# Attention memory and feed-forward kernel: the second feed-forward product with the activations stationary and 512 weight columns moving

## The chip, the cores and the metric

One core of one Trainium2 chip runs the whole program. The metric is the device time of one execution in microseconds. Three runs of the kernel before gave 767.05, 767.28 and 768.91; the median is 767.28.

## What is computed

8 batches, 8 heads, 576 tokens of 64 values a head, 32 memory slots; the feed-forward part has 512 inputs, 2048 hidden columns and 512 outputs. All in float32.

```python
a = softmax over tokens (phi)                      # b h s m
k_m = einsum('bhsm,bhsd->bhmd', a, k)
v_m = einsum('bhsm,bhsd->bhmd', a, v)
attn = softmax over m (q @ k_m.T / sqrt(64))       # b h s m
x = (attn @ v_m), heads side by side               # (4608, 512)
h = x @ w_in                                       # (4608, 2048)
sp = maximum(h, 0) + log1p(exp(-abs(h)))           # softplus
g = h * erf(sp)
return g @ w_out                                   # (4608, 512)
```

## The kernel before

**Folding.** `attn @ v_m @ w_in` is computed as `attn @ (v_m @ w_in)`: `vw` multiplies each head's 32x64 `v_m` with `w_in`, and the first product then contracts over 8 heads x 32 slots = 256 rows, in two groups of 128.

**Precision.** Most large products run in fp32r on split operands: `split` makes a high part (ScalarE, L110) and the remainder (VectorE, L111), and `products` forms three matmuls, high x high, high x low, low x high. Batch 0 keeps its first product, and the first 8 steps (`WHOLE`) keep their second product, in plain fp32 with one operand each; in the trace a plain fp32 matmul stands as two records.

**Weights.** `w_in` and `w_out` arrive as 64-bit words in 8 pieces of 1 MB each. `decode_1` and `decode_2` rebuild the floats: a clamp (VectorE L133), two conversions (ScalarE L136, L137), and two bit operations (VectorE L160, L163). `split_wo` later splits `w_out` for the fp32r steps.

**Steps.** `ORDER` lists 128 steps: 16 half batches `u` of 288 tokens, each with 8 steps `c` of 256 hidden columns. In step i:

- `ffn1(i, j)`, j = 0, 1 (L396): 6 matmuls each, vw stationary (128 hidden columns), 288 attention columns moving, into a bank `psh`; VectorE copies it to `h` (L405).
- `softplus` (L413) and, for four steps together, `erf` (L416) on ScalarE; the grouping saves activation table loads.
- `g_split` (L427 to L429) on VectorE, four steps later: e times h, its high part, its low part.
- `ffn2(i - 6, d)` (L444), d = 0 to 3: w_out stationary (128 output columns), g moving (288 tokens), 6 matmuls each, into one of four banks `pso`. After step c = 7 of a half batch ScalarE moves the four banks out (L469) and SyncE stores them (L472). The output is transposed, `outT`.

**The next batch's preparation** is hung on the steps by `at_slot`: the token softmax of phi (`phi_max`, `phi_sub`, `phi_exp`, `phi_sum`), the memory products (`kmvm`, L269, and `block_diag`, L285), `scores` (L302), the slot softmax (`sm_max`, `sm_exp`, `sm_norm`, `sm_back`), and four `vw_pair` (L302, then the split at L110 and L111). Batch 0's preparation stands ahead of step 0, together with the first decodes; this and the steps of batch 0 are called the front here.

**What sets the order.** The program is a list `prog` of (function, arguments); `merge` spreads side tasks between the four `ffn2` of a step. Each engine's instructions may then move only within `WINDOW` of that order: for TensorE freely in the first 16 steps (`HEAD`), then one, that is strictly in order; for VectorE 12, then 4; for ScalarE free, then 4. Loads are issued by SyncE when a buffer of their pool comes free (`room`, `fill`); `FIRST` gives the order of the earliest loads. kv has a ring of 3 buffers, q and phi one each, the weights 8. TensorE's results use 8 banks: two for `psh`, two for all small products (`psa`), four for `pso`.

```python
FIRST = "wo phiT phiT phi raw raw raw start q start wo wo wo wo".split()
...
lhsT=x[:, d * P : (d + 1) * P],   # ffn2: w_out
rhs=y[:, j, :],                   # ffn2: g, 288 tokens
```

## Time and profile before

| what | us |
|---|---|
| median of three runs | 767.28 (767.05 to 768.91) |
| span of the profiled execution, first to last instruction | 764.4 |
| TensorE busy | 728.3 |
| TensorE weight loads busy | 645.1 |
| VectorE busy | 515.9 |
| ScalarE busy | 433.8 |
| GpSimd busy | 0.7 |

The profile holds one execution and its span; the time of that execution around its span is not listed apart, so the span is set beside the median, which is 2.9 us longer. Times are us from the span's start. In groups of instructions, "x1920" counts records and "ns" is the mean length of one; matmuls are pipelined, so their lengths overlap, and the distance from start to start is what one costs. "PE" is TensorE, "PEld" its weight loads, "DVE" VectorE, "ACT" ScalarE, "POOL" GpSimd, "SPq" the queue in which SyncE issues DMAs. In a stretch of the timeline "x8" is eight instructions in a row, and the bracket names the idle time before them and what ended it.

### The profile page before, as it was taken

How to read it: one execution, taken by the hardware profiler on the slowest of the kernel's cores; microseconds unless marked ns; L12 is line 12 of the kernel's file. 1: busy time of each engine (PE TensorE's matmuls, PEld its weight loads, DVE VectorE, ACT ScalarE, POOL GpSimd, SP SyncE). 2: the span in 40 equal slices, each digit the busy share in tenths (PEclk: the TensorE clock that was granted, in tenths of full speed). 3: DMA queues.
4: the chain of work that ended last, by engine and by line, in shares of the span. 5: the costliest groups of instructions: out<-in, count | busy, mean ns of one | idle time of the engine just before them, and what ended most of it. 6: DMA issues, size and time to landing. Idle time of an engine off the chain costs nothing.

```text
span 764.4 us, 14301 instructions
## 1 busy us (share of the span) xinstructions
PE 728.3 (95%) x6016; PEld 645.1 (84%) x6016; DVE 515.9 (67%) x975; ACT 433.8 (57%) x704; POOL 0.7 (0%) x6
## 2 busy tenths in 40 slices
PE   2679899999999999999999999999999999999998
PEld 1245667699989999899999999989998999889998
DVE  3599867776668656777568746776577757667552
ACT  3679785565553746466454755556355755546450
POOL 0000000000000000000000000000000000000000
PEclk9999999999999999999999999999999999999999
DMA  8995042205201250004201151014401011000000
GB/s 295 389 384 245 1 155 63 63 5 180 66 32 33 69 173 32 20 21 154 96 32 32 48 171 47 18 32 126 124 32 32 17 48 32 33 2 32 1 32 32
DMA packets 34367, 64.88 MB, mean 85 GB/s; under 512 B 3072, under 2 KB 22016, under 8 KB 33280
## 3 DMA queue, kind: packets, MB, share of 16 engines
q1 hardware_dynamic: 34304, 63.98, 25.0%
q8 instruction: 47, 0.77, 0.5%
q14 instruction: 16, 0.13, 0.1%
HBM read 54.53 MB, written 9.44 MB: 84 GB/s over the span
## 4 chain that ended last, share of the span: by engine, by line
PE 83%; DVE 8%; ACT 7%; DMA 2%; issue 1%; SPq 0%; ACTq 0%
PE pso L444 50%; PE psh L396 24%; PE psa L302 5%; PE psa L269 3%; DMA phiT<-phiT 1%; DVE w_in L160 1%; ACT w_out L137 1%; ACT e L416 1%; ACT w_out L136 1%; PE psa L285 1%; DVE h L405 1%; DVE w_in L163 1%; ACT e L413 1%; DMA outT<-ot 1%; ACT L413 1%
## 5 line engine op out<-in xcount | busy, mean ns | idle before, releaser
L444 PE MATMUL pso<-g_hi,wo 128*128 128x288 f32 x1920 | 403.6, 295 | 0.1
L444 PEld LDWEIGHTS pso<-g_hi,wo 128*128 128x128 f32 x1920 | 315.0, 188 | 9.3 <-issue 8.3
L444 PE MATMUL pso<-g_lo,wo 128*128 128x288 f32 x960 | 283.4, 295 | 0.0
L444 PEld LDWEIGHTS pso<-g_lo,wo 128*128 128x128 f32 x960 | 180.4, 188 | 2.6 <-issue 1.7
L413 ACT ACTIVATE e<-h 128x576 f32<-128x576 f32 x128 | 86.9, 684 | 155.6 <-DVE h L405 155.2
L405 DVE COPY h<-psh 128x288 f32<-128x288 f32 x256 | 113.9, 450 | 15.7 <-PE psh L396 15.3
L427 DVE TENSOR_TENSOR e<-e,h 128x576 f32<-128x576 f32 x120 | 89.0, 743 | 43.3 <-ACT e L416 43.3
L396 PE MATMUL psh<-at_hi,vw_hi 128*128 128x288 f32 x448 | 101.2, 307 | 0.3 <-ACT at_hi L110 0.3
L396 PE MATMUL psh<-at_lo,vw_hi 128*128 128x288 f32 x448 | 95.7, 295 | 0.4 <-DVE at_lo L111 0.4
L396 PE MATMUL psh<-at_hi,vw_lo 128*128 128x288 f32 x448 | 95.7, 295 | 0.0
L429 DVE TENSOR_TENSOR g_lo<-e,g_hi 128x576 fp32r<-128x576 f32 x120 | 90.1, 751 | 0.5
L396 PEld LDWEIGHTS psh<-at_hi,vw_hi 128*128 128x128 f32 x448 | 70.4, 188 | 22.5 <-issue 16.1
L416 ACT ACTIVATE e<-e 128x576 f32<-128x576 f32 x128 | 80.1, 679 | 0.4
L428 DVE CAST g_hi<-e 128x576 fp32r<-128x576 f32 x120 | 54.4, 453 | 36.0 <-PE pso L444 34.4
L111 DVE TENSOR_TENSOR vw_lo<-psa,vw_hi 128x512 fp32r<-128x512 f32 x56 | 38.4, 686 | 59.1 <-ACT vw_hi L110 59.0
L396 PEld LDWEIGHTS psh<-at_lo,vw_hi 128*128 128x128 f32 x448 | 71.8, 188 | 0.6 <-DVE at_lo L111 0.6
L396 PEld LDWEIGHTS psh<-at_hi,vw_lo 128*128 128x128 f32 x448 | 71.9, 188 | 0.0
L469 ACT ACTIVATE ot<-pso 128x288 f32<-128x288 f32 x60 | 23.8, 407 | 48.4 <-DMA outT<-ot 29.0
L396 PE MATMUL psh<-at,vw 128*128 128x288 f32 x128 | 39.9, 446 | 10.1 <-DVE at L368 6.0
L396 PEld LDWEIGHTS psh<-at,vw 128*128 128x128 f32 x128 | 24.4, 203 | 23.0 <-DVE at L368 6.9
L413 ACT ACT_TABLE_LOAD x33 | 42.3, 1283 | 0.6
L416 ACT ACT_TABLE_LOAD x33 | 42.3, 1283 | 0.5
(65 smaller groups left out, 561.2 us busy)
## 6 DMA issues: line engine op xcount, KB each, us to landing
kv<-kv SPq DMA_DIRECT2D x32, 512.0 KB, 4.8
q<-qT SPq DMA_DIRECT2D x16, 576.0 KB, 3.9
outT<-ot SPq DMA_DIRECT2D x60, 144.0 KB, 1.8
w_in<-w_in SPq DMA_DIRECT2D x8, 1024.0 KB, 12.1
w_out<-w_out SPq DMA_DIRECT2D x8, 1024.0 KB, 12.7
phiT<-phiT SPq DMA_DIRECT2D x16, 288.0 KB, 3.1
phi<-phi SPq DMA_DIRECT2D x8, 512.0 KB, 5.4
kv<-kv SPq DMA_DIRECT2D x32, 64.0 KB, 4.5
```

The source lines that it names most:

```text
L111: nc.vector.tensor_tensor(out=lo, in0=src, in1=hi.bitcast(F32), op=ALU.subtract)
L269: nc.tensor.matmul(out=ps[M * j : M * (j + 1), 0, :], lhsT=a[:ln, c, (4 * g + j) * M : (4 * g + j + 1) * M], rhs=kvt[j][:ln, c], start=(c ...
L302: nc.tensor.matmul(out=ps[par][p * M : (p + 1) * M, :], lhsT=w[rows, p, :], rhs=x[rows, p, :], start=True, stop=True,)
L396: nc.tensor.matmul(out=ps, lhsT=x[:, g, j * P : (j + 1) * P], rhs=y[:, g, :], start=(k + g == 0), stop=(k == len(parts) - 1 and g == NG - 1),)
L405: nc.vector.tensor_copy(out=st["h", i][:, j], in_=ps)
L413: nc.scalar.activation(e, st["h", i], AF.Softplus)
L416: nc.scalar.activation(st["e", i], st["e", i], AF.Erf)
L427: nc.vector.tensor_tensor(out=g, in0=g, in1=st.pop(("h", i)), op=ALU.mult)
L428: nc.vector.tensor_copy(out=hi, in_=g)
L429: nc.vector.tensor_tensor(out=lo, in0=g, in1=hi.bitcast(F32), op=ALU.subtract)
L444: nc.tensor.matmul(out=o, lhsT=x[:, d * P : (d + 1) * P], rhs=y[:, j, :], start=(first and j + k == 0), stop=(last and j == 1 and k == len ...
L469: nc.scalar.activation(t, o, AF.Identity)
```

## The change

**The second product** swaps its operands. A step is now one 128-column slice k of the 2048 hidden columns for a whole batch of 576 tokens (`ORDER` lists batch and k, again 128 steps). `ffn1(i, half)` fills the two halves of one `h` row of 576. `ffn2(i, d)` takes 128 tokens of g as the stationary operand and moves 512 columns of w_out, 3 matmuls for each of four token tiles d, into four banks of 128x512, which are stored once a batch. The output is no longer transposed.

**The 64 leftover tokens** of a batch (576 = 4 x 128 + 64) are copied by GpSimd from g's high and low parts into `rest`, side by side for an even and an odd batch, and `ffn2_rest` multiplies the joined 128 tokens: four chunks of 12 matmuls, in the first four steps after the odd batch (`REST_TAIL`: in the last six rounds of the program). Batch 0's leftovers are kept in fp32 (`rest_f`) and split by `rest_split`.

**Batch 0** runs its whole second product in plain fp32 (`WHOLE = NK`, 16 steps), on the decoded w_out in place; the w_in pieces are wanted every second step, not every step.

**Banks and buffers.** One pool of four banks serves `psh`, `psa` and the leftovers' `psr`. kv, phi and q (from batch 1 on) share four `raw` buffers. The ring of `h` has five tiles instead of six.

**The front.** `FIRST` loads phiT, phi, kv and q of batch 0 before any weight; the first decode stands after the scores; both halves' scores and softmax come before step 0. `WINDOW` in the front is 3 for VectorE and 4 for ScalarE. `merge` rounds up, so side tasks stand one `ffn2` earlier. `phi`, `kmvm` and `scores` of the next batch are hung on other steps.

```diff
-    FIRST = "wo phiT phiT phi raw raw raw start q start wo wo wo wo".split()
-    HEAD = 16
+    FIRST = "phiT phiT raw raw raw raw start start start wo wo wo wo wo".split()
+    HEAD = NK
-        mybir.EngineType.DVE: (12, 4),
-        mybir.EngineType.Activation: (10000, 4),
+        mybir.EngineType.DVE: (3, 4),
+        mybir.EngineType.Activation: (4, 4),
-    WHOLE = NPR
+    WHOLE = NK
+    REST_TAIL = {0: (0,), 1: (1,), 3: (2,), 5: (3,)}
-    HB, EB = 6, 5
-    ORDER = [(u, c) for u in range(NU) for c in range(NPR)]
+    HB, EB = 5, 5
+    ORDER = [(b, k) for b in range(B) for k in range(NK)]
...
-    ps_h = ctx.enter_context(tc.tile_pool(name="ps_h", bufs=2, space=PSUM))
+    ps_s = ctx.enter_context(tc.tile_pool(name="ps_s", bufs=4, space=PSUM))
     ps_o = ctx.enter_context(tc.tile_pool(name="ps_o", bufs=1, space=PSUM))
-    ps_a = ctx.enter_context(tc.tile_pool(name="ps_a", bufs=2, space=PSUM))
...
     def g_split(i):
+        for x, y in enumerate((hi, lo)):
+            nc.gpsimd.tensor_copy(out=rest[:, k, x, cols], in_=y[:, NT * P :])
...
     def ffn2(i, d):
-        for j in range(2):
-            w = [wf[c][:, j]] if i < WHOLE else [wo[c][:, x, j] for x in range(2)]
-            parts = products(w, g)
-            for k, (x, y) in enumerate(parts):
-                    lhsT=x[:, d * P : (d + 1) * P],
-                    rhs=y[:, j, :],
+        w = [wf[k // 2][:, k % 2]] if i < WHOLE else [x[:, k % 2] for x in wo[k // 2]]
+        parts = products([t[:, d * P : (d + 1) * P] for t in g], w)
+        for n, (y, z) in enumerate(parts):
+                lhsT=y,
+                rhs=z,
...
+    def ffn2_rest(b, q):
+        if q == 0:
+            st["o_rest"] = ps_s.tile([P, DM], F32, name="psr", tag="ps")
+        for k in range(4 * q, 4 * q + 4):
+            parts = products(
+                [rest[:, k, n, :] for n in range(2)], [x[:, k % 2] for x in wo[k // 2]]
+            )
...
+    def store(o, rows, on_vector):
+        t = ost.tile([P, DM], F32, name="ot")
+                nc.scalar.activation(t, o, AF.Identity)
+            nc.sync.dma_start(out=out[r : r + ln], in_=t[n * ln : (n + 1) * ln])
...
-    prog = [(phi_max, 0, 0), (phi_max, 0, 1), d[0], (phi_sub, 0), (phi_exp, 0)]
+    prog = [(phi_max, 0, 0), (phi_max, 0, 1), (phi_sub, 0), (phi_exp, 0)]
+    prog += [(scores, 0), (scores, 1), d[0], (sm_max, 0), (sm_max, 1), (sm_exp, 0), (sm_exp, 1), d[1]]
+    prog += [(sm_norm, 0), (sm_back, 0), (vw, 0), (sm_norm, 1), (sm_back, 1)]
...
-            m = (n + 1) * len(b) // len(a)
+            m = -(-(n + 1) * len(b) // len(a))
```

**Where instructions move.** The first place is TensorE in the middle of the program: one step's first product (psh) and the second product of the step six earlier (pso), before:

```order
L396 MATMUL psh<-at_hi,vw_hi 128x288 x2
L396 MATMUL psh<-at_lo,vw_hi 128x288 x2
L396 MATMUL psh<-at_hi,vw_lo 128x288 x2
L444 MATMUL pso_1504<-g_hi,wo 128x288
L444 MATMUL pso_1504<-g_lo,wo 128x288
L444 MATMUL pso_1504<-g_hi,wo 128x288 x2
L444 MATMUL pso_1504<-g_lo,wo 128x288
L444 MATMUL pso_1504<-g_hi,wo 128x288
```

and the like step of the changed kernel:

```order
L390 MATMUL psh<-at_hi,vw_hi 128x288 x2
L390 MATMUL psh<-at_lo,vw_hi 128x288 x2
L390 MATMUL psh<-at_hi,vw_lo 128x288 x2
L447 MATMUL pso_1307<-wo,g_hi 128x512 x2
L447 MATMUL pso_1307<-wo,g_lo 128x512
```

The first product is as it was; a bank of the second now receives three matmuls of 512 columns in a step where it received six of 288.

The second place is TensorE in the second step of batch 2, where a chunk of leftovers (psr), a vw pair (psa from w_in) and the next phi (psa from diag) stand in one step; changed kernel:

```order
L447 MATMUL pso_1307<-wo,g_hi 128x512 x2
L447 MATMUL pso_1307<-wo,g_lo 128x512
L304 MATMUL psa<-w_in_359,vm_101 32x512 x8
L447 MATMUL pso_1327<-wo,g_hi 128x512 x2
L447 MATMUL pso_1327<-wo,g_lo 128x512
L228 MATMUL psa<-diag,ones 128x128 x2
L447 MATMUL pso_1331<-wo,g_hi 128x512 x2
L447 MATMUL pso_1331<-wo,g_lo 128x512
L468 MATMUL psr<-wo,rest 128x512 x12
```

Before, a vw pair stood at the end of a step, after all four pso, with banks of its own:

```order
L444 MATMUL pso_983<-g_hi,wo 128x288 x2
L444 MATMUL pso_983<-g_lo,wo 128x288
L444 MATMUL pso_983<-g_hi,wo 128x288
L302 MATMUL psa<-w_in_451,vm_104 32x512 x8
L396 MATMUL psh<-at_hi,vw_hi 128x288 x2
```

It has moved ahead of most of its step's second product, and shares four banks with psh and psr.

The third place is VectorE at the start (pmx: the maxima of phi; psm, prs: sums and reciprocals; sc: scores), before:

```order
L133 TENSOR_SCALAR w_in<-w_in 128x1024
L215 TENSOR_REDUCE pmx_138<-phiT 128x1
L215 TENSOR_REDUCE pmx_143<-phiT 128x1
L216 TENSOR_SCALAR pmx_138<-pmx_138 128x1
L160 SCALAR_TENSOR_TENSOR w_in<-w_in 128x1024
L216 TENSOR_SCALAR pmx_143<-pmx_143 128x1
L163 SCALAR_TENSOR_TENSOR w_in_171<-w_in 128x4x256
L237 TENSOR_TENSOR phi<-phi,psa 128x1024
```

and changed:

```order
L217 TENSOR_REDUCE pmx_136<-phiT 128x1
L217 TENSOR_REDUCE pmx_141<-phiT 128x1
L218 TENSOR_SCALAR pmx_136<-pmx_136 128x1
L218 TENSOR_SCALAR pmx_141<-pmx_141 128x1
L239 TENSOR_TENSOR phi<-phi,psa 128x1024
```

The three steps of the first weight's decode have left the chain to phi; they now stand between the two halves' softmax.

More of the change, by code (lines that the diff above doesn't have):

```diff
@@ L41, in tile_memory_attention_then_erf_softplus_ffn @@
     w_out: bass.AP,
-    outT: bass.AP,
+    out: bass.AP,
 ):
@@ L166, in decode_2, with room_wf @@
         )
+    def room_wf():
+        st["wf"] = raw_pool.tile([P, 2, DM], F32, name="wf", tag="raw")
     def split_wo(c):
-        wo[c] = wop.tile([P, 2, 2, DM], F32R, name="wo", tag="wo")
-        split(wo[c][:, 0], wo[c][:, 1], wf.pop(c))
+        t = wop.tile([P, 2, 2, DM], F32R, name="wo", tag="wo")
+        split(t[:, 0], t[:, 1], wf.pop(c))
+        wo[c] = [t[:, x] for x in range(2)]
     def load_phiT(b, g):
@@ L296, in heads @@
     def heads(w, x, n):
-        ps = [ps_a.tile([P, n], F32, name="psa") for _ in range(2)]
+        ps = [ps_s.tile([P, n], F32, name="psa", tag="ps") for _ in range(2)]
         for p in range(NP_):
@@ L461, in ffn2 @@
-        if i == NS - 1:
-            if d % 2 == 0:
-                st["ot"] = el.tile([P, 2, U], F32, name="h", bufs=HB)
-            t = st["ot"][:, d % 2]
-        else:
-            t = ost.tile([P, U], F32, name="ot")
-        if (u, 0) == ORDER[i - c]:
+                    lhsT=y,
+                    rhs=z,
+                    start=(k + n == 0),
+                    stop=(k == NK - 1 and n == len(parts) - 1),
+                )
+        if q == NK // 4 - 1:
+            store(st.pop("o_rest"), [((b + x) * S - REST, REST) for x in range(2)], 0)
@@ L498, in merge @@
+        for x in range(2):
+            for n, f in ((6, scores), (7, sm_max), (7, sm_exp), (9, sm_norm), (10, sm_back)):
+                at_slot(e + n + (3 + (f in (scores,))) * x, f, 2 * b + x)
+        for p in range(4):
+            at_slot(o + 13 + 4 * p, vw_pair, b, p)
+    for b in range(1, B - 1, 2):
+        for q in range(NK // 4):
+            at_slot((b + 1) * NK + q, ffn2_rest, b, q)
     def merge(a, b):
```

259 lines of the change are left out of this document (124 added, 135 removed).

## The prediction

> **What bounds the kernel now.** I read the page first, then the stages, then the chain of waits in order of time, then TensorE's timeline around single steps. Busy time by engine and the granted clock, from the page:
>
> ```profile
> PE 728.3 (95%) x6016; PEld 645.1 (84%) x6016; DVE 515.9 (67%) x975; ACT 433.8 (57%) x704; POOL 0.7 (0%) x6
> ...
> PEclk9999999999999999999999999999999999999999
> ```
>
> Stages (columns: length, then busy us of PE, PEld, DVE, ACT, POOL, then clock, DMA share, GB/s):
>
> ```profile
> 0.00:40.00 40.00, 17.11 (x139) 7.59 (x140) 18.86 (x32) 20.78 (x35) 0.70 (x6) 1.00 0.98 342
> 40.00:80.00 40.00, 33.47 (x206) 18.88 (x204) 37.13 (x55) 34.50 (x48) 0.00 (x0) 0.96 0.73 286
> ...
> 600.00:700.00 100.00, 100.00 (x862) 93.60 (x861) 68.62 (x137) 56.97 (x94) 0.00 (x0) 1.00 0.10 31
> ```
>
> There are two regimes. In the front TensorE waits, first for loads, then (40 to 80) for VectorE, busy 37.13 of 40. Later TensorE never stops and VectorE has a third of its time free. The chain, in order of time, gives TensorE's price list (start, length):
>
> ```profile
> 403.30 3.17 PE pso L444 x24
> ...
> 490.40 3.17 PE pso L444 x24
> ...
> 739.10 22.22 PE pso L444 x168
> ```
>
> 24 second-product matmuls of 288 columns take 3.17 us, so one takes **132 ns**, and 168 at the end, with little beside them, the same. The same place of two successive batches lies 87.1 us apart. Of that 384 x 132 = 50.7 us are the second product, 192 x 132 = 25.3 the first (same size, same pitch), 11.1 the small matmuls of the next batch. Nothing is idle, so after the front only fewer or cheaper matmuls help.
>
> **The second product.** The multiply count is unchanged: a batch has 16 x 4 x 3 = 192 matmuls of 512 columns, plus 48 for the joined leftovers of two batches, so 216 a batch in place of 384; 216 x 512 = 384 x 288 columns. All therefore hangs on the pitch of a 512-column fp32r matmul, which no row shows. The nearest rows, TensorE's timeline (start, length):
>
> ```profile
> 120.78 2.10 PE L396 MATMUL psh<-at,vw 128*128 128x288 f32 x8
> 122.72 2.10 PE L444 MATMUL pso<-g,wf 128*128 128x288 f32 x8
> ...
> 417.97 0.61 PE L226 MATMUL psa<-diag,ones 128*128 128x128 f32 x4
> 418.33 0.51 PE L396 MATMUL psh<-at_hi,vw_hi 128*128 128x288 f32 x2
> ```
>
> In plain fp32 eight records start within 1.94 us, 242.5 ns each, and a program's matmul is two records, 485 ns or 3.67 times 132. If that is four passes (my reading), a column costs at most 0.421 ns, so 288 columns need 121.2 ns and fp32r pays 10.8 ns beyond them. Three readings of the 10.8:
> - paid once per matmul: 512 x 0.421 + 10.8 = **226.3 ns**;
> - hidden under a longer move, as it seems to be in fp32: 215.5 ns;
> - part of the column rate: 512 x 132 / 288 = 234.7 ns.
>
> I take the first. The four fp32 records of L226, each with its own weight load, follow each other within (418.33 - 417.97) / 3 = 120 ns at most, so the load alone does not set 132; and an extra per instruction is the value between the ends. Both ends stay in the range.
>
> The Trainium skill, "TensorE: Matmul & The Clock Gate", section "Back-to-back issue gap", gives an isolated warm gap of N / 2.4 + 2.5 ns: 122.5 at 288 columns, where this trace has 132, and 215.8 at 512. By it the sum would be that of the second reading.
>
> Batch 0 now runs the whole second product in fp32: 128 records x (242.5 x 512 / 288 = 431 ns) = 55.2 us, against 128 x 0.2425 + 192 x 0.132 = 56.4 before. Over the kernel TensorE's second product goes from 2880 x 0.132 + 31.0 = 411.2 us to 1536 x 0.2263 + 55.2 = 402.8. It breaks even at 232 ns.
>
> **Leftover tokens.** 16 x 2 copies of 128x64 a batch move to an idle POOL. Prices around them:
>
> ```profile
> L405 DVE COPY h<-psh 128x288 f32<-128x288 f32 x256 | 113.9, 450 | 15.7 <-PE psh L396 15.3
> ...
> L111 DVE TENSOR_TENSOR vw_lo<-psa,vw_hi 128x512 fp32r<-128x512 f32 x56 | 38.4, 686 | 59.1 <-ACT vw_hi L110 59.0
> ...
> L110 ACT ACTIVATE vw_hi<-psa 128x512 fp32r<-128x512 f32 x56 | 30.5, 596 | 11.1 <-PE psa L302 11.1
> ...
> L469 ACT ACTIVATE ot<-pso 128x288 f32<-128x288 f32 x60 | 23.8, 407 | 48.4 <-DMA outT<-ot 29.0 <-PE pso L444 18.9 <-PE psh L396 0.5
> ...
> masks.py:199 POOL TENSOR_SCALAR_AFFINE_SELECT ident<-ident 128x128 f32<-128x128 f32 x1 | 0.3, 294 | 0.1
> ```
>
> At 294 ns or less a copy is at most 9.4 us of POOL time a batch, hidden under TensorE's batch. Even if each kept VectorE out for its length, VectorE's 0.686 x 87.1 = 59.8 us a batch would become 69, still below TensorE's 25.3 + 216 x 0.2263 + 11.1 = 85.3. I cost it at nothing; the last step's copies feed a leftover chunk in the same step, three times, some tenths of a us.
>
> The Trainium skill, "SBUF — State Buffer", section "Who interferes with whom", says that a VectorE instruction with two SBUF inputs contends with a GpSimd instruction that reads SBUF. No row here shows POOL reading beside VectorE; by it the 69 would stand.
>
> **Stores.** Eight evictions of 407 ns a batch become 4.5 of 596 (the row of that size): 3.3 to 2.7 us of an engine with 43% free. Each bank is next written a first product (1.6 us) later than its last matmul; cover enough. Two output buffers still hold ScalarE for the DMA, softplus and erf queued behind, as in the 29.0 us above that cost TensorE nothing. The ring of h falls from six tiles to five: step k's tile is freed by its product in step k + 4, which VectorE runs before the copy that needs it in step k + 5, so this costs nothing.
>
> **Shared tiles.** kv, q and phi now share four buffers, and the second pair of kmvm stands one step behind the first, not two. Its last kv load starts when the first pair is read. Cover: 3 x 0.68 + 1.6 + 0.68 = 4.3 us. Landing times from the table of DMA issues:
>
> ```profile
> kv<-kv SPq DMA_DIRECT2D x32, 512.0 KB, 4.8
> q<-qT SPq DMA_DIRECT2D x16, 576.0 KB, 3.9
> ```
>
> ```profile
> 409.64 0.39 SPq L207 DMA_DIRECT2D q<-qT  x1
> ```
>
> With 0.4 us to issue, as q's takes, that is 0 (q's landing, a lone load like this) to 0.9 us late, seven times: 0 to 6 us; I take 1.
>
> **The front.** VectorE's timeline, the chain into the first product, and the decode's prices:
>
> ```profile
> 8.92 0.70 DVE L133 TENSOR_SCALAR w_in<-w_in 128x1024 f32<-128x1024 f32 x1 [7.92 <-DMA w_in<-w_in]
> 9.64 1.53 DVE L215 TENSOR_REDUCE pmx<-phiT 128x1 f32<-128x576 f32 x2
> ...
> 11.14 1.22 DVE L160 SCALAR_TENSOR_TENSOR w_in<-w_in 128x1024 int32<-128x1024 int32 x1
> 12.27 0.15 DVE L216 TENSOR_SCALAR pmx<-pmx 128x1 f32<-128x1 f32 x1
> 12.39 1.22 DVE L163 SCALAR_TENSOR_TENSOR w_in<-w_in 128x1024 int32<-128x1024 int32 x1
> ...
> 27.84 0.97 DVE L337 STREAM_TRANSPOSE sc<-psa 128x288 f32<-128x288 f32 x2 [9.25 <-PE psa L302]
> ```
>
> ```profile
> 16.73 2.52 PE L269 MATMUL psa<-kv,phi 128*32 128x128 f32 x40 [3.03 <-ACT phi L259]
> ...
> 38.41 4.21 PE L396 MATMUL psh<-at,vw 128*128 128x288 f32 x8 [5.95 <-DVE at L368]
> ...
> 64.75 4.15 PE L444 MATMUL pso<-g,wf 128*128 128x288 f32 x16 [0.54 <-DVE g L422]
> ```
>
> ```profile
> 140.07 0.53 PE L396 MATMUL psh<-at_hi,vw_hi 128*128 128x288 f32 x2 [0.27 <-ACT at_hi L110]
> ```
>
> A megabyte of w_in no longer stands ahead of phiT (2.9 us at the first stage's 342 GB/s) and its decode no longer sits between the maxima (1.2 us): the chain is 4 us earlier, the first score transpose at 23.8. Now both halves' softmax and one decode come before the first product. Lengths by size, from the groups of instructions:
>
> ```profile
> L237 DVE TENSOR_TENSOR phi<-phi,psa 128x1024 f32<-128x1024 f32 x8 | 9.8, 1220 | 3.4 <-PE psa L226 3.3
> ...
> L422 DVE TENSOR_TENSOR g<-e,h 128x576 f32<-128x576 f32 x8 | 5.9, 745 | 0.0
> ```
>
> Ten operations of 0.75 and a decode of 3.1 (L133 + L160 + L163: 0.70, 1.22, 1.22) are about 11 us of VectorE: the first product starts at **34.6**, not 38.4. Then six steps without a second product, bound by VectorE: four decoded pieces (12.4), 12 copies of 0.45 (5.4), two g of 0.745 (1.5) and batch 1's phi (two maxima of 0.75, 1.22 and small ones: 4) = 23.3, about 24 (26.3 before): 58.6. Ten steps follow, bound by TensorE since w_in's eight pieces are now spread over the whole batch: 8 x 0.2425 + 4 x 0.862 + 0.3 = 5.7 each, 57, and 4 for batch 1's small matmuls. Before, the like stretch of 75.3 held 65 of matmuls (10 x 1.94 of the first product, 31.0 + 6.3 of the second, 8 of small ones); I keep 9 of those 10 us of loss: 61 + 9 = 70. Batch 1 starts at **128.6**, say 128, against 140.07. Bounds: 119 with no loss, 140 if VectorE's unchanged instruction mix sets it all.
>
> **From there to the end**, 764.4 - 140.07 = 624.3 us now. Seven batches: 7 x (50.7 - 192 x 0.2263) = -50.7. Four leftover sets: 4 x 48 x 0.2263 = +43.5. Six steps of batch 0 still due, in fp32: 24 x 0.862 - 144 x 0.132 = +1.7. Small matmuls that the new order leaves for later (two vw pairs, less one half's scores):
>
> ```profile
> 400.44 1.09 PE L302 MATMUL psa<-w_in,vm 64*32 64x512 f32 x16
> 401.46 0.53 PE L396 MATMUL psh<-at_hi,vw_hi 128*128 128x288 f32 x2
> ```
>
> at 1.1 and 0.75 each, +1.5. Load wait +1. Together -3.0: 621.3. Sum: 128 + 621.3 = 749.3 us of span. The profiled span of 764.4 lies 2.9 below the median of 767.28; adding that, **752 us**.
>
> **Rivals.**
> - *The extra hides under longer moves* (215.5 ns). Speaking for it: the 242.5 ns records show no such extra. Against: the load alone fits in 120. 1344 + 192 matmuls at 10.8 ns less: -16.6, so **735**. The skill's rule above gives this.
> - *The column sets the price* (234.7 ns). For: no row separates columns from instructions. 1536 x 8.4 = +12.9: **765**, the front's gain all that is left.
> - *VectorE's queue reaches TensorE*, slower. Place: the vw pairs, 28 of them. From the list of waits (total, times, longest):
>
> ```profile
> DVE vw_lo L111 <- ACT vw_hi L110: 59.0, 26, 3.2
> ...
> PEld psh L396 <- DVE h L405: 6.2, 6, 1.9
> ```
>
> VectorE stands 2.3 us for ScalarE's half of the split, with h copies queued behind. The pair's two banks, h's two and for four steps the leftovers' one now come out of four in common, so the next first product waits for 2.3 + 2 x 0.69 + 2 x 0.45 = 4.6 us of work under a cover of 12 x 0.226 + 1.0 = 3.7: 0.9 x 28 = 25 us, **777**. It decides from (767.3 - 752) / 28 = 0.55 us a pair. Against it: the same sum leaves 0.4 us today, and TensorE's 6.2 us of such waits all lie in the front.
>
> **How the numbers follow.** Chances: forecast 0.43, hidden extra 0.22, column price 0.20, queue 0.15. The range takes the first three with part of the front's bounds and leaves out the queue and the lowest fronts: 733 to 768. Within 0.3% of 767.28 (765.0 to 769.6, about what a measurement can tell from no change) falls half of the column case; its other half, the forecast and the hidden extra are faster, 0.75; same 0.10; slower 0.15.
>
> **What would show it.** Right: L447 runs of 12 in 2.72 us, batches 85 us apart, batch 1's first product near 128, POOL near 40 us busy with no TensorE wait on it. A run of 12 in 2.59 is the second reading, in 2.82 the third. The queue case would show TensorE idle before psh, released by h copies. The front is wrong if batch 1 starts after 135, and the whole if batches lie over 87 us apart.

## The result, and the profile after

| | before | after |
|---|---|---|
| median, us | 767.16 (4 runs, 765.88 to 768.91) | 771.5 (4 runs, 770.15 to 773.18) |
| ratio, 95% interval | | 1.0062 [1.0041, 1.0083] |
| profiled execution: span, us | 764.4 | 767.8 |

The change made the kernel slower by 0.6%. The forecast was 752, faster; the range ended at 768.

The page's rows of the kernel after, to set beside the first two rows quoted in the prediction:

```profile
PE 725.4 (94%) x4672; PEld 549.2 (72%) x4672; DVE 511.4 (67%) x963; ACT 459.2 (60%) x696; POOL 88.2 (11%) x246
...
PEclk9997999999999999999999999999999999999999
```

TensorE has 1344 instructions fewer and is busy 3 us less, in a span 3.4 us longer. The fourth slice's granted clock has fallen to 7 tenths, where it was 9. The stages (columns: length, then busy us of PE, PEld, DVE, ACT, POOL, then clock, DMA share, GB/s), with the piece of the front that the prediction had put at 24 us, from the first product to the first second product, as the last row:

```profile
0.00:40.00 40.00, 20.02 (x150) 10.82 (x151) 20.09 (x39) 17.15 (x33) 0.70 (x6) 1.00 0.99 343
40.00:80.00 40.00, 30.92 (x213) 17.98 (x212) 28.27 (x45) 29.07 (x47) 2.81 (x4) 0.87 0.75 268
600.00:700.00 100.00, 100.00 (x656) 81.63 (x655) 67.38 (x131) 57.31 (x88) 13.94 (x40) 1.00 0.11 36
...
34.50:67.10 32.60, 23.52 (x149) 15.25 (x149) 23.88 (x42) 27.39 (x40) 1.41 (x2) 0.84 0.83 300
```

From 40 to 80 VectorE was busy 37.13 of 40 us before and is busy 28.27 now: it is no longer what the front hangs on. In the last row it is busy 23.88 us, just the 23.3 that the prediction added up, but the piece lasts 32.6. TensorE's timeline through it and at batch 1 (start, length; in brackets the idle time ahead and what ended it):

```profile
34.11 6.73 PE L390 MATMUL psh<-at,vw 128*128 128x288 f32 x16 [1.36 <-DVE srs L353]
...
52.25 1.21 PE L390 MATMUL psh<-at,vw 128*128 128x288 f32 x4 [1.73 <-DVE phi L244]
55.76 0.77 PE L304 MATMUL psa<-w_in,vm 64*32 64x256 f32 x16 [2.30 <-DVE w_in L161]
59.86 2.52 PE L271 MATMUL psa<-kv,phi 128*32 128x128 f32 x40 [3.33 <-ACT phiT L249]
63.57 3.61 PE L390 MATMUL psh<-at,vw 128*128 128x288 f32 x8 [1.19 <-ACT vw L319]
...
67.12 2.31 PE L447 MATMUL pso<-w_out,g 128*128 128x512 f32 x5
...
132.27 2.10 PE L390 MATMUL psh<-at,vw 128*128 128x288 f32 x8
134.00 0.64 PE L390 MATMUL psh<-at_hi,vw_hi 128*128 128x288 f32 x2
...
137.70 0.53 PE L390 MATMUL psh<-at_lo,vw_hi 128*128 128x288 f32 x2 [1.81 <-DVE at_lo L114]
...
138.50 5.11 PE L447 MATMUL pso<-w_out,g 128*128 128x512 f32 x8
```

The first product starts at 34.1, as forecast (34.6), but the first second product at 67.1 (58.6 forecast, 64.75 before) and batch 1 at 134.0 (128 forecast, 140.07 before). The bracketed waits from 52 us on add up to 8.6 us: 5.1 belong to batch 1's preparation (phi, phiT), the rest to a decode (w_in) and an eviction (vw) queued around it. The same eight fp32 records of the first product take 3.61 us at 63.57 and 2.10 at 132.27. The last row's eight second-product records take 5.11 us, where eight at full pace take 3.6: after these waits TensorE runs at half rate for a while. The last section comes back to when it does so and when not.

The steady part, from the chain of waits in order of time:

```profile
221.26 2.75 PE pso L447 x12
...
227.67 2.73 PE psr L468 x12
```

Twelve second-product matmuls of 512 columns in 2.75 us are 229.2 ns each, between the prediction's first (226.3) and third (234.7) reading. From the start of a batch to that of the next but one it is 173.8 us (315.57 to 489.33) and 173.0 (397.06 to 570.11), so 86.5 to 87 a batch: before 87.1, forecast 85.3. From batch 1's start to the end it is now 767.8 - 134.0 = 633.8 us; 624.3 before, 621.3 forecast. (The expectations below have 633.4 and 134.4 for these two: the same first matmul, taken 0.4 us later.)

The copies of the leftover tokens and the split of the vw pairs, from the groups of instructions:

```profile
L431 POOL CAST rest<-g_hi 128x64 fp32r<-128x64 f32 x112 | 41.8, 373 | 383.2 <-DVE g_hi L428 380.9
...
L114 DVE TENSOR_TENSOR vw_lo<-psa,vw_hi 128x512 fp32r<-128x512 f32 x56 | 37.7, 684 | 32.0 <-ACT vw_hi L113 32.0
...
L431 POOL CAST rest<-g_lo 128x64 fp32r<-128x64 f32 x112 | 34.2, 305 | 133.4 <-DVE g_lo L429 112.8
```

The copies take 373 and 305 ns, more than the 294 assumed, on an engine that has time. VectorE's wait for ScalarE's half of the split fell from 59.0 to 32.0 us, and behind 150 us TensorE waits for an h copy only once, for 0.6 us: the rival of VectorE's queue did not come about.

So there were five suspects: the front's order; the pitch (the time from one matmul's start to the next); ScalarE held by the stores; the small matmuls, which now stand inside the second product; and POOL. The experiments take them one by one. All ratios are to the kernel before, timed beside each version, and stand beside 1.0062 of the changed kernel.

### The profile page after: what moved, and what is told of

It reads as the page before. It is cut to its first block, busy times and chain, and to the rows that moved or that the text cites. A ratio compares the mean times of both kernels' runs of the same rounds, so it can differ in the third digit from the quotient of the medians.

```text
span 767.8 us, 12022 instructions
## 1 busy us (share of the span) xinstructions
PE 725.4 (94%) x4672; PEld 549.2 (72%) x4672; DVE 511.4 (67%) x963; ACT 459.2 (60%) x696; POOL 88.2 (11%) x246
## 4 chain that ended last, share of the span: by engine, by line
PE 81%; ACT 5%; DVE 4%; DMA 2%; issue 1%; SPq 0%; DVEq 0%; ACTq 0%
PE pso L447 44%; PE psh L390 23%; PE psr L468 6%; PE psa L304 5%; PE psa L271 2%; DMA out<-ot 2%; ACT L407 1%; ACT e L410 1%; ACT e L407 1%; ACT L410 1%; DVE h L399 1%; ACT w_out L140 0%; ACT ot L484 0%; PE psa L228 0%; PE psa L287 0%
## 5 line engine op out<-in xcount | busy, mean ns | idle before, releaser
L447 PE MATMUL pso<-wo,g_hi 128*128 128x512 f32 x896 | 284.6, 399 | 0.0
L447 PEld LDWEIGHTS pso<-wo,g_hi 128*128 128x128 f32 x896 | 157.5, 188 | 51.4 <-issue 28.5
L447 PE MATMUL pso<-wo,g_lo 128*128 128x512 f32 x448 | 176.1, 393 | 0.0
L447 PEld LDWEIGHTS pso<-wo,g_lo 128*128 128x128 f32 x448 | 84.1, 188 | 19.4
L390 PEld LDWEIGHTS psh<-at_hi,vw_hi 128*128 128x128 f32 x448 | 77.7, 188 | 14.7 <-issue 2.9
L431 POOL CAST rest<-g_hi 128x64 fp32r<-128x64 f32 x112 | 41.8, 373 | 383.2 <-DVE g_hi L428 380.9
L429 DVE TENSOR_TENSOR g_lo<-e,g_hi 128x576 fp32r<-128x576 f32 x112 | 84.0, 750 | 1.7
L114 DVE TENSOR_TENSOR vw_lo<-psa,vw_hi 128x512 fp32r<-128x512 f32 x56 | 37.7, 684 | 32.0 <-ACT vw_hi L113 32.0
L447 PE MATMUL pso<-w_out,g 128*128 128x512 f32 x112 | 53.1, 613 | 2.4 <-ACT e L410 2.0
L431 POOL CAST rest<-g_lo 128x64 fp32r<-128x64 f32 x112 | 34.2, 305 | 133.4 <-DVE g_lo L429 112.8
L304 PE MATMUL psa<-w_in,vm 64*32 64x512 f32 (+1 forms) x576 | 38.0, 561 | 10.1 <-DVE ssm L351 7.2
```

Of the source, the lines that this page charges most:

```text
L114: nc.vector.tensor_tensor(out=lo, in0=src, in1=hi.bitcast(F32), op=ALU.subtract)
L304: nc.tensor.matmul(out=ps[par][p * M : (p + 1) * M, :], lhsT=w[rows, p, :], rhs=x[rows, p, :], start=True, stop=True,)
L390: nc.tensor.matmul(out=ps, lhsT=x[:, g, k % 4 * P : (k % 4 + 1) * P], rhs=y[:, g, :], start=(n + g == 0), stop=(n == len(parts) - 1 and g ...
L429: nc.vector.tensor_tensor(out=lo, in0=e, in1=hi.bitcast(F32), op=ALU.subtract)
L431: nc.gpsimd.tensor_copy(out=rest[:, k, x, cols], in_=y[:, NT * P :])
L447: nc.tensor.matmul(out=o, lhsT=y, rhs=z, start=(k + n == 0), stop=(k == NK - 1 and n == len(parts) - 1),)
```

## Experiments

### Three output buffers

```
-    ost = ctx.enter_context(tc.tile_pool(name="ost", bufs=2))
+    ost = ctx.enter_context(tc.tile_pool(name="ost", bufs=3))
```

> The changed kernel with three output buffers (pool ost) in place of two, nothing else. Theory (stores hold ScalarE): at a batch's end the third store waits for the DMA of the first, ScalarE stands 1.3 to 1.7 us in it, and behind it stand the copies of km and vm, for which the scores of the first half wait on TensorE (0.3 to 0.9 us, in batches 2 to 5). With a third buffer the four runs of 16 score matmuls that took 1.31, 1.61, 1.77 and 1.16 us fall to about 0.75 each, and at the end of the kernel the last store but one no longer waits: -2.5 to -3 for the scores and -1 to -2.6 for the tail, so 0.9943 of the changed kernel, 767 us. Rival (the leftovers' bank psr is one of the four shared ones, and its holding is what the scores wait for): the score runs stay as they are, only the tail moves, 769.5 us or more.

Measured: 766.79 us, ratio 1.0000 [0.9988, 1.0012]. The mechanism in the changed kernel, at the end of batch 2's second product, first on ScalarE, then on TensorE:

```profile
348.34 0.69 ACT L407 ACTIVATE e<-h 128x576 f32<-128x576 f32 x1
350.71 0.60 ACT L484 ACTIVATE ot<-pso 128x512 f32<-128x512 f32 x1 [1.69 <-DMA out<-ot]
351.34 0.22 ACT L294 ACTIVATE vm<-psa 64x64 f32<-64x64 f32 x1
```

```profile
350.64 0.67 PE L304 MATMUL psa<-q,km 64*32 64x288 f32 x2
351.61 0.71 PE L304 MATMUL psa<-q,km 64*32 64x288 f32 x14 [0.30 <-ACT vm L294]
```

The third store has no buffer until the first store's DMA is done; ScalarE stands 1.69 us, the last copy of vm behind it, and the scores stop after two matmuls. With three buffers, at the same place:

```profile
345.13 1.16 ACT L484 ACTIVATE ot<-pso 128x512 f32<-128x512 f32 x2
346.18 0.20 ACT L291 ACTIVATE km<-psa 64x64 f32<-64x64 f32 x1
```

```profile
348.78 0.71 PE L304 MATMUL psa<-q,km 64*32 64x288 f32 x16
```

Three stores go without a wait for a buffer, km and vm come before the fourth, and the sixteen score matmuls run through in 0.71 us. Batch 1 to the end takes 628.3 us in place of 633.8. Of these 5.5 us the buffer did not give all: the four score runs are shorter by 3.1 us (1.31, 1.68, 1.84 and 1.16 from the first start to the last end, against 0.71 to 0.72 each), but 1.5 us are the half rate at batch 1's first step, which this trace does not have although TensorE waits the same 1.81 us there (its eight records take 3.60 us, not 5.11). The rival (the leftovers' bank) falls: that bank is held as before, and the score runs are short. At the kernel's end the expectation was too high: the last store still waits for a buffer, on VectorE, in the changed kernel and with three:

```profile
764.23 0.69 DVE L481 COPY ot<-pso 128x512 f32<-128x512 f32 x1 [2.92 <-DMA out<-ot]
```

```profile
759.24 0.69 DVE L481 COPY ot<-pso 128x512 f32<-128x512 f32 x1 [2.41 <-DMA out<-ot]
```

The same kernel once more:

> A second look at the changed kernel with three output buffers, in the same call as the others, for its trace beside theirs: batch 1 to the end 628 us (633.4 in the changed kernel), span 761 to 764.

765.85 us, span 764.0, batch 1 to the end 630.0. Here the eight records at batch 1 take 4.74 us, nearly as in the changed kernel, and the four score runs are again 3.1 us shorter. By the ratios the buffer is worth 4.8 us; the traces show 3.1 of them in the score runs and about 0.6 at the kernel's end, and the rest is within the intervals.

### Small work at the ends of steps

```
-            m = -(-(n + 1) * len(b) // len(a))
+            m = (n + 1) * len(b) // len(a)
```

> The changed kernel with the merge that rounds down, as the kernel before had it, so that a step's one small task (a vw pair, a half's scores, kmvm) stands behind the last of its four second-product blocks and ahead of the next step's first product, not between two blocks. Theory (interruptions cost): each entry of small matmuls into the second product costs some 90 ns and each restart some 98 ns, 52 to 62 of them, 10.7 us, of which 6.6 was there before; with the small work at a step's end the restart is into the first product, as before, and 3 to 5 us come back: 767 us (0.994 to 0.996 of the changed kernel). Rival (the cost is that of the small matmuls themselves, wherever they stand): within 1 us of 771.5. A second rival: the small work's results (scores, vw) come later by a block or two and the next step waits for them: slower by 1 to 3 us.

769.18 us, 1.0031 [1.0018, 1.0043]: 2.4 us better, but not where the theory had it. Batch 1 starts at 129.8 in place of 134.0, and from there to the end it takes 634.4 us, 0.6 more than in the changed kernel (whose 633.8 hold 1.5 us of half rate that this trace does not have). The list of TensorE's waits from 150 us on (total, times, longest) has a new one, for stores at the end of a batch:

```profile
PE pso L447 <- ACT ot L484: 3.2, 4, 1.1
```

Without these 3.2 us, and with the half rate taken out of the 633.8, some 1 us would be left of the 3 to 5 expected. The theory that the restarts inside the second product cost several us is not borne out by the time: what was gained was gained in the front, and nothing behind it. With three buffers as well:

> The changed kernel with three output buffers and with the small work at the steps' ends. If the two gains lie in different places, as their traces say (the buffers: 5.5 us from batch 1 to the end; the step ends: batch 1 starts at 129.9 in place of 134.4, nothing behind it, since four second products of a batch's first step then wait 3.2 us in all for stores), they add and the third buffer takes these 3.2 away too: ratio to the kernel before 1.0062 - 0.0062 - 0.003 - up to 0.003, so 0.993 to 0.997, 761 to 764 us. Rival (the earlier start of batch 1 is given back later, as in the run with batch 1 prepared later): 766 us, no better than the buffers alone.

763.8 us, 0.9965 [0.995, 0.998]: better than either edit, and as much as the two gains add up to (0.9969). Where in the program they lie was not read for this version.

### The front alone, and the change without it

In the kernel before, the first batch's loads put in front, as the change does:

```
-    FIRST = "wo phiT phiT phi raw raw raw start q start wo wo wo wo".split()
+    FIRST = "phiT phiT phi raw raw raw start q start wo wo wo wo wo".split()
...
-    prog = [(phi_max, 0, 0), (phi_max, 0, 1), d[0], (phi_sub, 0), (phi_exp, 0)]
+    prog = [(phi_max, 0, 0), (phi_max, 0, 1), (phi_sub, 0), (phi_exp, 0)]
...
-    prog += d[1:2]
...
-    prog += [(scores, 0), (sm_max, 0), (vw, 0, 0), (sm_exp, 0)]
+    prog += [(scores, 0), d[0], (sm_max, 0), (sm_exp, 0), d[1], (vw, 0, 0)]
```

> The kernel before with the change's front alone: the first batch's phiT, phi and kv are loaded ahead of w_in, and w_in's first decode stands behind the first scores. Theory (the front's first part is worth what it seemed): the chain phiT, phi, kmvm, scores is 3 to 4 us earlier, the first product starts at 35 in place of 38.4, and some of it is kept to batch 1, which starts at 137 in place of 140: 764 us, 0.996 of the kernel before. Rival (what follows is bound by VectorE's and ScalarE's total work in the front, not by when it begins): the first product earlier, batch 1 at 140 as before, 767 us. The other side: the decoded piece that the first vw needs comes later, and the first product does not move: 767 to 769 us.

762.5 us, 0.9946 [0.9932, 0.996]. On TensorE:

```profile
35.33 3.70 PE L396 MATMUL psh<-at,vw 128*128 128x288 f32 x8 [4.03 <-DVE at L368]
...
137.41 0.50 PE L396 MATMUL psh<-at_hi,vw_hi 128*128 128x288 f32 x2 [0.56 <-DVE h L405]
```

Much as expected: the first product 3.1 us earlier, batch 1 2.7 us earlier, 4.0 us in the medians. In the changed kernel the opposite edit (w_in's first piece back in front of phiT, its decode back between the maxima):

> The changed kernel without its front: w_in's first piece loaded ahead of phiT and decoded between the maxima, as before. If the front is worth here what it is worth to the kernel before (4.1 us): 775 to 776 us, first product at 38, batch 1 at 137 to 138. Rival (in the changed kernel, where two halves' softmax stand ahead of the first product and batch 1's preparation comes early, the gain is lost on the way to batch 1): 771 to 773 us. The two theories differ in whether batch 1's start moves with the first product's.

773.97 us, 1.0114 [1.0091, 1.0137]: 4.0 us slower than the changed kernel by the ratios, the first product at 36.8 and batch 1 at 137.1.

```profile
36.83 6.51 PE L390 MATMUL psh<-at,vw 128*128 128x288 f32 x16 [6.02 <-DVE srs L353]
...
137.11 0.64 PE L390 MATMUL psh<-at_hi,vw_hi 128*128 128x288 f32 x2
```

The loads in front are worth about 4 us in either kernel. The rest of the change, without this piece, costs 8 to 9.

### The pitch by columns

Each matmul of 512 columns split in two of 256, each of the leftovers' in 384 and 128:

```
+            for x in range(0, DM, 256):
...
-                out=o,
+                    out=o[:, x : x + 256],
...
-                rhs=z,
+                    rhs=z[:, x : x + 256],
```

> The changed kernel with each 512-column matmul of the second product split in two of 256 columns (same stationary operand loaded for each), and each of the leftovers' in one of 384 and one of 128. For the price of columns alone; a look at the trace, not a version. By a fixed extra of 10.8 ns per matmul and 0.421 ns a column (the prediction's reading): 118.6 ns at 256, 172.5 at 384. By the line through the two measured points (132 at 288, 229.3 at 512: 0.435 ns a column and 6.7 fixed): 118 at 256, 174 at 384, 62 at 128 unless the weight load sets a floor. By the weight load as a floor (bounded by 120 ns in the prediction): 128 columns take 105 to 120. The second product then has 2 x 118 = 236 in place of 229: the time rises by 1344 x 7 ns = 9 us and for the leftovers by 192 x 50 = 10 at most, 780 to 792 us.

790.06 us in one run. From the chain of waits:

```profile
231.93 3.38 PE psr L470 x24
...
282.32 2.83 PE pso L448 x24
```

24 matmuls of 256 columns take 2.83 us, 117.9 ns each. Two of them, 235.8 ns, move what one of 512 moves in 229.2, so the fixed part is 6.6 ns, and a column costs (229.2 - 6.6) / 512 = 0.435 ns; 288 columns come to 131.8, as measured. The prediction's split of 10.8 and 0.421 is wrong in both parts. A pair of 384 and 128 takes 281.7 ns (3.38 us for 12 pairs), 46 more than two of 256, where the line gives the same. If 384 cost 173.6 by that line, 128 would cost 108; but in the trace the move of 384 is followed after 225 to 230 ns and the move of 128 after some 60. So the pair has a price beyond its columns, and whether the short move or the weight load beside it makes it is not shown.

### Batch 1 prepared later

```
-        e = o + (2 if b == 1 else 0)
+        e = o + (4 if b == 1 else 0)
```

and its softmax closed up behind, so that its last piece stays at step 15.

> The changed kernel with the preparation of batch 1 begun two steps later (its phi maxima at step 4 in place of 2, kmvm at 7 and 8, scores at 10 and 12) and closed up behind, so that its last piece still stands at step 15. Theory (the six-step part of the front is slow because batch 1's phi work stands in VectorE's and ScalarE's order between the decodes and h copies that the first product waits for, 3.3 us of VectorE idle behind TensorE's phi maximum product among it): the first second product at 61 to 63 us in place of 67.5, and of the 5 us some 2 to 4 are kept to batch 1, which starts at 130 to 132 in place of 134.4: 767.5 to 769.5 us. Rival (the sum of work of VectorE and ScalarE up to batch 1 sets its start, in whatever order): first second product earlier by 2 to 5, batch 1 at 134 as before, 771 us. The other side: the closed-up softmax is late for batch 1's first product, which then waits: 773 or more.

771.34 us, 1.0071 [1.0058, 1.0084]: the mechanism of the third case, at a time nearer to the rival's. The first second product comes at 64 and batch 1 starts at 129.1, 5 us earlier than in the changed kernel; then its first step stands. TensorE and ScalarE there:

```profile
138.89 0.85 PE L390 MATMUL psh<-at_hi,vw_hi 128*128 128x288 f32 x2 [8.62 <-ACT at_hi L113]
...
140.85 4.29 PE L447 MATMUL pso<-w_out,g 128*128 128x512 f32 x8
```

```profile
123.77 0.38 ACT L319 ACTIVATE vw<-psa 128x256 f32<-128x256 f32 x1 [7.24 <-PE psa L304]
...
127.00 1.28 ACT L345 ACT_TABLE_LOAD   x1
128.30 0.68 ACT L345 ACTIVATE sc<-sc 128x576 f32<-128x576 f32 x1
```

ScalarE stood idle 7.24 us for a weight pair's matmuls while the exponential of batch 1's second half (L345) was queued behind that pair's evictions, though its input had been ready from about 121. So the order on ScalarE, and not the sum of its work, made the second half late. That led to the next edit: a step later only, and the second half's exponential in step 12, which holds no weight pair.

```
-        e = o + (2 if b == 1 else 0)
+        e = o + (3 if b == 1 else 0)
...
+            if b == 1:
+                for n, f in ((9, scores), (9, sm_max), (9, sm_exp), (11, sm_norm), (11, sm_back)):
+                    at_slot(o + n + 2 * x, f, 2 * b + x)
+                continue
```

Together with three output buffers:

> The changed kernel with three output buffers and batch 1 prepared one step later at its start (phi maxima at step 3), the second half's exponential in step 12, where no weight pair stands ahead of it on ScalarE. Theory (the later preparation shortened the front by 5 us, and it was lost only in the 8.6 us that batch 1's first step waited for the second half's softmax, whose exponential stood behind the weight pair's evictions): batch 1 at 130 to 133 and no wait over 3 us in its first step; from there 628 us; 761 to 764 us. Rival (the wait moves with the sum of VectorE's and ScalarE's work in the front): batch 1's second half waits 4 us or more again, 766 us or more.

758.33 us, **0.9897 [0.9879, 0.9915]**: the best version, below both kernels. TensorE:

```profile
59.36 3.87 PE L390 MATMUL psh<-at,vw 128*128 128x288 f32 x8 [3.97 <-ACT vw L319]
...
65.59 3.60 PE L447 MATMUL pso<-w_out,g 128*128 128x512 f32 x8
...
129.63 0.64 PE L390 MATMUL psh<-at_hi,vw_hi 128*128 128x288 f32 x2
...
131.42 3.60 PE L447 MATMUL pso<-w_out,g 128*128 128x512 f32 x8
```

Batch 1 starts at 129.6, its first step has no wait, and the eight second-product records after it take 3.60 us in place of 5.11. From there to the end it is 756.3 - 129.6 = 626.7 us. With two buffers, as in the changed kernel:

> The changed kernel with two output buffers, as it was, and batch 1 prepared a step later with the second half's exponential in step 12: the one edit by which the run with three buffers went from 1.000 to 0.990 of the kernel before. If it and the buffers are independent: 1.0062 - 0.0103 = 0.996, 763 us, batch 1 at 130. Rival (the gain needs the third buffer, whose absence holds ScalarE at the end of batch 0 just where batch 1's weight pairs come): 0.999 or more, 766 us or more.

763.22 us, 0.9945 [0.9928, 0.9962]: the buffer is not needed for it. And with three buffers and only the softmax closed up, the phi work begun at step 2 as in the change:

> Three output buffers; batch 1's phi work begins at step 2 as in the changed kernel, but its softmax is closed up as in the best run (scores at 9 and 11, the second half's exponential in step 12). Which half of that edit gave its 8 us? If the later phi chain (front shorter by work moved off it): first second product at 67, batch 1 at 133 to 135, 764 to 766 us. If the earlier exponential of the second half (its place ahead of the weight pair on ScalarE, no wait in batch 1's first step, no half-rate matmuls after it): first second product at 67, but batch 1 at 130 to 131 without a wait, 758 to 760 us.

763.17 us, 0.9958 [0.9941, 0.9974]. TensorE at batch 1:

```profile
134.27 0.65 PE L390 MATMUL psh<-at_hi,vw_hi 128*128 128x288 f32 x2
...
135.28 0.42 PE L390 MATMUL psh<-at_hi,vw_hi 128*128 128x288 f32 x2
...
136.07 3.60 PE L447 MATMUL pso<-w_out,g 128*128 128x512 f32 x8
```

Batch 1 starts as late as in the changed kernel, but without the wait: each half of the edit gives a part, 0.0042 of the time (3.2 us) the earlier exponential, 0.0061 (4.7 us) the later phi chain. I had expected one of them to have it all.

All three edits at once (buffers, step ends, preparation):

> The three edits together: three output buffers, small work at step ends, batch 1 prepared a step later. If all are independent: batch 1 at 128 to 130, from there 627 to 629, 758 to 761 us, below both kernels by 0.8% and more. If the front is bound by the sum of its work, batch 1 at 130 as with the step ends alone and 762 to 764 us.

763.53 us, 0.9958 [0.9941, 0.9974]: worse than without the step ends. In its trace batch 1 starts at 129.1 as in the best version, but takes 91.0 us to batch 2 in place of 86.5, and the pair of batches behind it 172.3 in place of 171.5. There TensorE waits 1.2 us for a scaled diagonal of the next phi (ScalarE L222) and 2.1 us for a weight pair's remainder (VectorE L114), and eight second-product records behind the second wait take 5.29 us in place of 3.60. So the small work at step ends, which gained in the front alone, loses here.

### Wider windows, and no copies on POOL

The order of batch 0 left as loose as before:

```
-        mybir.EngineType.DVE: (3, 4),
-        mybir.EngineType.Activation: (4, 4),
+        mybir.EngineType.DVE: (12, 4),
+        mybir.EngineType.Activation: (10000, 4),
```

> The changed kernel with the order of instructions in batch 0 left as loose as the kernel before had it (an instruction of VectorE may be passed by up to 12 later ones in place of 3, of ScalarE by any number in place of 4). Theory (strict order holds VectorE and ScalarE behind waits of batch 1's preparation): the idle 3.3 us of VectorE near 47 to 51 goes and the first second product comes 2 to 4 us earlier; batch 1 at 130 to 133, 768 to 770 us. Rival (the scheduler, free, puts early what is due late, and the total of work decides): within 1 us of 771.5, or slower.

775.49 us, 1.0121 [1.0104, 1.0138]: slower. From TensorE's waits between 34 and 135 us:

```profile
PE psh L390 <- DVE at L362: 13.3, 1, 13.3
```

Left free, the softmax of batch 0 falls behind other work and the first product starts at 42.4. The first second product then comes at 60.9, 6.2 us earlier than in the changed kernel, but batch 1 only at 141.2, 7.2 us later: what the loose order gains in the six steps it loses in the ten behind them. So loosening the whole front does not help; whether a part of the strict order costs is not shown.

Without POOL's copies (the leftover rows of the output leave out their data):

> The changed kernel without POOL's copies of the leftover tokens (their tile is set to zero once, so the leftover rows of the output, the last 64 tokens of each batch, leave out their second product's data; its matmuls still run). Prediction's step (the copies are hidden): 770 to 773 us, VectorE's and ScalarE's means unchanged. Rival (POOL's 88 us of reading and writing slow VectorE's two-input instructions and so the path): VectorE's split and subtract means fall by 2% or more, and the time by 2 to 5 us.

770.36 us, 1.0056 [1.0042, 1.0069], the changed kernel's own time within the intervals; VectorE's lines read as with the copies:

```profile
L428 DVE TENSOR_TENSOR e<-e,h 128x576 f32<-128x576 f32 x112 | 83.3, 744 | 77.0 <-ACT e L411 77.0
...
L115 DVE TENSOR_TENSOR vw_lo<-psa,vw_hi 128x512 fp32r<-128x512 f32 x56 | 37.7, 684 | 32.5 <-ACT vw_hi L114 32.5
```

744 and 684 ns with the copies and without. (Only the first of these lines has both inputs in SBUF; vw_lo's first input is TensorE's bank.) On VectorE POOL's 76 us of reading and writing cost nothing that shows in the time. POOL itself pays, as the trace of the changed kernel shows:

```profile
726.09 0.75 DVE L427 TENSOR_TENSOR e<-e,h 128x576 f32<-128x576 f32 x1
726.23 0.70 POOL L431 CAST rest<-g_hi 128x64 fp32r<-128x64 f32 x1 [2.40 <-DVE g_hi L428]
...
727.79 0.45 DVE L399 COPY h<-psh 128x288 f32<-128x288 f32 x1
727.93 0.24 POOL L431 CAST rest<-g_lo 128x64 fp32r<-128x64 f32 x1 [1.00 <-DVE g_lo L429]
```

A copy that runs alone or beside an h copy takes 237 to 240 ns. The 31 copies that start while VectorE multiplies e by h, with two inputs in SBUF, all end 95 to 99 ns after that multiply, and take 626 to 764 ns. The contention that the prediction quoted from the Trainium skill, "SBUF — State Buffer", section "Who interferes with whom", is there, then, and falls on an engine that has time.

## Why the prediction was wrong, step by step

The forecast of the span was 749.3, the profiled span is 767.8: 18.5 us.

1. **The leftovers' matmuls and the instruction count** (right). 2.73 / 12 = 227.5 ns apiece, 192 of them 43.7 us, against 43.5 forecast.
2. **The pitch** (a term mis-sized). 229.2 ns against 226.3 for 1344 matmuls, 227.5 for the leftovers' 192: 3.9 + 0.2 = 4.1 us. The step that failed is "a column costs at most 0.421 ns" taken as the fp32r rate: that is what fp32 records show, and here 0.435 was measured for fp32r. The second product's gain is then 411.2 - 1344 x 0.2292 - 43.7 - 128 x 0.43 = 4.4 us in place of 8.4. The rule of the Trainium skill, "TensorE: Matmul & The Clock Gate", section "Back-to-back issue gap", gave 215.8 at 512 columns; it does not hold for fp32r here. A warm fp32 record of 512 columns, two passes by that rule, would be 1024 / 2.4 + 2.5 = 429 ns, an estimate from that page; 429 to 430 was measured.
3. **"Two output buffers still hold ScalarE ... cost TensorE nothing"** (failed). True before, where the copies of km and vm were done some 4 us ahead of the scores (at 365.6 and 369.8 us, for one) and TensorE has no wait behind 150 us; the new order of the work put them, and through them the scores, right behind a store. 3.1 us in the score runs, the same in both traces with the third buffer; 4.8 by the ratios.
4. **"Six steps without a second product, bound by VectorE"** (failed). VectorE's work was sized right (23.9 against 23.3) but was not the bound: the piece took 33.0 us, not 24. ScalarE, which I did not add up, is busy 27.4 of the 32.6 us of the row, more than the 24 by itself, and batch 1's phi chain goes VectorE, ScalarE, TensorE, VectorE, ScalarE, TensorE, and stands in each engine's order ahead of the decodes. The ten steps after it took 66.9 (70 forecast). Batch 1 started 6 us later than forecast; 4.7 us of it came back when the phi chain began a step later. That the chain costs batch 1 its start is so shown; that it makes the six steps slow is shown in part only: of their 9.0 us over the forecast 1.6 came back with the chain one step later and 3.5 with two. How the rest divides between ScalarE's sum of work, the order and TensorE's half rate stays open.
5. **The first step of batch 1** (not in the sum). The second half's softmax came 2 us late, and in the profiled execution TensorE then ran at half rate, 1.5 us more. With the earlier exponential both are gone; by the ratios that is worth 3.2 us. The half rate is in part luck: it did not follow the same wait in every trace.
6. **The ring of h, shared tiles, POOL** (right in what they cost): behind batch 1's start no wait of TensorE on POOL or h is worth a us, though POOL is busy 88 us where "near 40" was named: 240 copies of 238 ns would be 57, and what they wait for VectorE is the rest. The load wait of 1 us that was taken did not come. The last store waits for its buffer, which the sum did not have: 6.3 us from the last matmul's start to the end, 3.4 before.

In the traces items 2 to 5 make 4.1 + 3.1 + 6.0 + 3.5 = 16.7 us and the late last store 2.9; less the load wait of 1 that is 18.6, for the 18.5 that were missing. As a check: the version with items 3 and 5 and most of 4 undone has a span of 756.3, 7.0 above the forecast: 4.1 of pitch, 1.6 for batch 1 at 129.6 in place of 128 and 2.4 for the last store (5.8 from the last matmul's start), less 1, make 7.1.

The marks that the prediction set itself were too wide apart: batch 1 at 134 is inside 135, the batches at 86.5 to 87 are inside 87, and yet the sum was out by 19 us, since each was nearly missed. Of the rivals none was it. The slower side came about by instructions that stood behind a waiting one on ScalarE, at a batch's end and in the front, and not by VectorE's queue at the vw pairs.

## What to carry to other kernels

Where a change moves work between engines in a start-up phase, adding up the busiest engine's time is not enough: follow each chain through every engine's queue, and ask of each instruction that waits for a DMA or for TensorE what stands behind it. A store in two buffers or an eviction pair can hold a softmax that is due, and one more buffer or one step in the order was worth as much or more here (3.7 to 4.8 us, and 9 us) than the whole new product (4.4 us). An unknown pitch is cheap to get beforehand: one kernel with the operands split in halves gives the fixed part and the rate apart.

## What the runs showed of the hardware that was not expected

- After a wait TensorE can run at half rate for some us. In the changed kernel fp32 records of 288 columns start 480 ns apart from 34.7 to 39 us and from 64.2 to 66.5, and 243 ns apart behind that; records of 512 columns 851 to 853 ns apart from 138.5 to 141.1 and 430 behind. Ahead of the last TensorE had stood for 0.2 and 1.8 us. Summed over the fp32 records of both products in the changed kernel, what they take beyond their full pace is 4.2 us, and in the one before 2.1, so a wait on TensorE can cost more than its own length. The Trainium skill, "TensorE: Matmul & The Clock Gate", section "Part 1: The HAM clock gate (the "warmup" mystery)", tells of such a half rate after an idle window of about 3.4 us, left again after about as much work; the trace agrees with the halving and with the length, and shows it after less idle time than that.
- Whether the half rate follows depends on where a wait falls. The same wait of 1.8 us in batch 1's first step was followed by it in three traces (eight records in 5.11, 4.58 and 4.74 us: changed kernel, without POOL's copies, three buffers once more) and not in two (3.60 and 3.59: three buffers, front undone). In all traces the granted clock changes only on a grid of 3.41 us. In the three the interval that holds most of the wait had TensorE busy for 0.41, 0.51 and 0.41 of it, and the clock is 0.5 in the next interval; in the two the wait is shared between two intervals, busy 0.68 and 0.73, and 0.54 and 0.88, and the clock stays. Two of the five traces are of one program, with three buffers, and differ here by 1.1 us.
- 12 pairs of fp32r moves of 384 and 128 columns take 3.38 us where 24 of 256 take 2.83: an uneven split costs 46 ns a pair.
- POOL's copies of 128x64 to fp32r took 373 ns in the mean for one source and 305 for the other, in the same shapes. Alone both take 238. 25 copies of the first and 6 of the second start during VectorE's multiply of e by h and wait for its end; that, and waits for some other instructions of VectorE, makes the means differ.
